# Window attention beside a GELU MLP: two one-bank PSUM tiles for the logits, one memset on another engine, and a new order of the pieces

## The chip, the cores and the metric

The kernel runs on one core of a Trainium2 chip. The metric is the device time of one execution in microseconds; several executions are timed and the median is given. One further execution is recorded by the hardware profiler; its trace is what the views below are taken from. Engines are called by their short names: PE (matmuls, and PEld for its weight loads), DVE, ACT, POOL and SP. SP and POOL, and now and then ACT, issue DMAs from their queues.

## The reference

For one sequence of 2048 rows of 640 columns, all in bf16:

```
xn  = layernorm(x)                                   # no gain or bias
q, k, v = split(xn @ wqkv)                           # 32 heads of 20 columns
logits[h, s, w] = q[h, s] . k[h, s - 2 w] / sqrt(20) # w = 0..7, masked where s - 2 w < 0
o[h, s] = sum_w softmax(logits)[h, s, w] * v[h, s - 2 w]
out = x + o @ wo + gelu(xn @ w1 + b1) @ w2 + b2      # w1: 640 x 1536, w2: 1536 x 640
```

## The kernel before

**Tiling.** The 2048 rows are four chunks n = 0..3 of 512 rows, each of four blocks of 128 rows. Normalised rows `xn` are turned so that the 640 columns lie on partitions (five tiles of 128). Everything on PE works on such turned chunks: 5 matmuls of 128x512 for each of 15 tiles of q, k, v (piece `pj`, line 333) and each of 12 tiles of the hidden layer (`f1`, line 614), and 12 + 5 matmuls for each of 5 output tiles (`t`, line 696). In chunk 0, q, k and v are made in halves and quarters of a chunk (`ga`, `gb`, `gd`, `ge`, `hj`; lines 346 and 377), so that work can begin before all of the chunk is loaded; in chunk 3 the outputs are not turned (`o`, line 652). ACT copies PE's results out of PSUM (`pc`, `hc`, `gc`), applies the GELU (`ge0_5` is tile 5 of chunk 0), makes `xn` for chunks 1 to 3 and takes the exponentials.

**Attention.** For each block j DVE multiplies q by eight shifted windows of k into `prod` (`qk`, line 430), folds the five column tiles by additions (`pa`, `pb`, lines 465 and 471), and PE sums each head's columns with a matrix of ones, `head_of`: piece `lg`, line 480, eight matmuls of 128x512 that make the logits tile `L`, 4 blocks x 32 heads on partitions, 8 windows x 128 rows in the free direction, 4 KB per partition. `L` is copied to SBUF as `e` (`cp`, lines 512 to 520); then come the mask (chunk 0 only), the maximum over windows and its subtraction (`m`, `mx`, DVE), the exponential (`ex`, ACT), the sum (`ss`, DVE), its reciprocal (`ri`, ACT), and the weights (`at`, DVE). DMAs on SP's queue spread the weights over the head's columns (`xe`, line 577). DVE multiplies them by windows of v (`av`, line 584) and adds up over windows (`ac`, partly by DMAs on POOL's queue, `ad`, `ot`).

**The softmax of chunk 0 goes in two parts** (`PARTS = (2, 1, 1, 1)`): each takes 64 of the 128 rows of every block. ACT copies the first part and DVE the second, and both parts of `L` reach over both halves of the windows, and so over both PSUM banks of the tile.

**PSUM.** Eight banks of 2 KB per partition: `psA` has four one-bank buffers (`pj`, `hj`, `f1`, most of `o`), `psO` two (`t`), and `psL` one buffer of two banks: the logits `L`, and at other times the idle matmuls that run before the data arrive, the bias transpose `tb`, and the first block of outputs in chunk 3.

**Loads at the start.** SP loads the rows of block 0, then wq, blocks 2 and 3, wk, chunk 1, wv and w1. ACT's queue loads block 1; DVE writes 16 columns of that block with zeros ahead of it (line 131), and the load has to wait for this write.

**What sets the order.** The program is written as some 600 small pieces, and `ORDER` lists them: each engine works through its own pieces in that order, and the queues of SP and POOL too. Nothing else reorders them. A piece waits by semaphores for what it reads, and for the buffer that it writes to be free. Pieces used in the text, all of chunk 0 unless said: `xn01a`, `xn01b` (DVE, the normalised block 1 in two parts), `tp01a` (PE, turns the first part), `lg0` (logits), `cp0a`, `cp0b`, `mask`; `pj1..` and `pj2..` (q, k, v of chunks 1 and 2) with the copies `pc1..`, `pc2..`; `hj210`, `hj211` with the copies `hc210`, `hc211`; `su`, `sq`, `rs`, `rc` (statistics of a later chunk's rows: two sums and the inverse root on ACT, `rc` the product -mean/std on DVE, line 252); `xn20`..`xn23` (normalised blocks of chunk 2, ACT, two buffers), `tc20`..`tc23` (DMA transposes of them, SP, line 291); `ut` and `ud` (the output tiles turned back and added to `out`).

Of the kernel before, what the change touches and what calls it, by code (L numbers as in the profile page):

```python
# [50 lines left out]
t002 xe00 ge0_9 pj123 pad21 su32 pb14 pj210 xe02 su31 pj203 xp1 pc210 su30 lg1 t042 pc203 av01 cp1b f10_10 ng3 f11_5  # L51
pj212 ge1_5 av00 ac01 pc123 f11_0 cp1a ge0_10 pj204 pad12 ge1_0 m1 pc212 ac00 pj211 sq32 av02 pj202 sq30 t003 pc211
pc204 pj221 pc202 mx1 pj223 av03 ex1 pj222 sq31 t043 pj214 ss1 pc222 pc221 f11_2 ac03 ri1 pj213 pc214 sq33 at1 pj220
ac02 pc213 xe11 rs3 xe13 pj201 pc220 xe10 rc3 ad01 pj224 pc201 xe12 pc223 ad00 pj200 f12_9 pc200 ot00 xn33 f12_3 ot01
xn31 tc33 av11 t004 tc31 t044 u00 pc224 t010 u04 ut00 av13 ac11 t011 xn32 t012 t013 ud00 f11_11 av12 t014 t030 u01
# [12 lines left out]
o330 ut24 ac32 o322 ud23 o313 ac33 o304 ad31 o331 ud24 o323 dl0 dh0 o314 ot31 dd0 o324 dl1 dh1 dd1 o332 dl2 o333 dh2
dd2 o334 ohi dl3 dlo dh3 dhi
# [4 lines left out]
def kernel(  # L74
# [44 lines left out]
    b_rt = consts.tile([P, P], BF16, name="b_rt")  # L119
    nc.gpsimd.memset(b_rt[:], 0.0)  # L120
# [10 lines left out]
    nc.vector.memset(x_sb[:, 1, 0:16], 0.0)  # L131
# [341 lines left out]
    def do_lg(n):  # L473
        L = psL.tile([P, W, P], F32, tag="L", name="L")
        tiles["L", n] = L
        ts = (range(KT), (0, 1, 4), (0, 4), (0,))[LEVEL[n]]
        for h in range(2):
            for t in ts:
                for j in range(BPC):
                    nc.tensor.matmul(  # L480
                        L[j * H : (j + 1) * H, W // 2 * h : W // 2 * (h + 1), :],
                        lhsT=head_of[:],
                        rhs=prod[:, j, W // 2 * h : W // 2 * (h + 1), t, :],
                        start=(t == 0),
                        stop=(t == ts[-1]),
                        skip_group_check=True,
                    )
# [24 lines left out]
    def do_cp(n, i):  # L512

        e = softmax_tile("e", n, [W, P], BF16)
        if PARTS[n] == 1:
            ws = slice(W // 2 * i, W // 2 * (i + 1))
            nc.scalar.copy(e[:, 0, ws, :], tiles["L", n][:, ws, :])
        else:
            cs, width = part(n, i)
            (nc.vector.tensor_copy if i else nc.scalar.copy)(e[:, i, :, :], tiles["L", n][:, :, cs])  # L520

# [335 lines left out]
```

## Time and profile before

| what | us |
|---|---|
| median of three runs | 206.66 (205.86 to 207.09) |
| the profiled execution | 205.97 |
| its span, from the first to the last instruction | 203.8 |
| DVE busy | 185.8 (91% of the span) |
| ACT busy | 128.9 (63%) |
| POOL busy | 29.3 (14%) |
| DMA moved | 27.31 MB, mean 134 GB/s |

The 2.2 us between the span and the execution's own time lie outside of the instructions. In a view's rows, times are microseconds from the start of the span: start, length, engine, line of the kernel, operation, tiles out<-in, shapes, how many instructions. A bracket at the end gives the idle time of the engine ahead of the row and what ended it. Matmuls overlap: a row's length reaches past the start of the next row, so that PE's pace is read from starts, not from lengths.

### The profile page before, as it was taken

What the parts mean: (1) busy time and instruction counts of PE and PEld (TensorE: products, weight loads), DVE (VectorE), ACT (ScalarE), POOL (GpSimd) and SP (SyncE); (2) the same over time, 40 slices, a digit from 0 to 9 for tenths busy, and PEclk for the clock granted to TensorE, in tenths of its full rate; (3) what the DMA queues carried; (4) which work ended last, traced back from release to release, by engine and by line L of the source; (5) the groups of instructions that cost most, each with busy time, mean ns of one, the idle gap of its engine ahead of it and who ended that gap; (6) DMA issues with size and microseconds to landing.
All of it is one profiled execution on the core that took longest, in us unless ns stands there. A gap on an engine that the chain in (4) does not pass through costs nothing.

```text
span 203.8 us, 2870 instructions
## 1 busy us (share of the span) xinstructions
PE 199.9 (98%) x1100; PEld 105.1 (52%) x1100; DVE 185.8 (91%) x160; ACT 128.9 (63%) x237; POOL 29.3 (14%) x34
## 2 busy tenths in 40 slices
PE   8999999999999999999999999999999999999994
PEld 3998456574544555444445544444434454444552
DVE  2889999699998999999999998999979999998871
ACT  5669899899896998657184445996379942230100
POOL 2000000000000400040420040000022713236210
PEclk9999999999999999999999999999999999999999
DMA  6997499900448781779399190003745899795851
GB/s 203 389 395 207 93 314 372 351 2 0 68 86 260 154 155 19 190 145 131 82 160 104 26 102 1 3 0 61 170 51 105 141 104 204 96 104 76 79 90 64
DMA packets 38430, 27.31 MB, mean 134 GB/s; under 512 B 25106, under 2 KB 34578, under 8 KB 38418
## 3 DMA queue, kind: packets, MB, share of 16 engines
q1 hardware_dynamic: 28016, 20.39, 35.3%
q0 software_dynamic: 10080, 6.56, 27.9%
q10 hardware_dynamic: 322, 0.20, 0.3%
q8 instruction: 8, 0.13, 0.3%
q14 instruction: 4, 0.03, 0.0%
HBM read 10.49 MB, written 4.59 MB: 74 GB/s over the span
## 4 chain that ended last, share of the span: by engine, by line
PE 84%; ACT 7%; DMA 4%; DVE 2%; SPq 1%; issue 1%
PE T L696 27%; PE hps L614 23%; PE pps L333 22%; PE lo L652 5%; DMA x_sb<-in_A_x_dram 4%; PE both L652 2%; DVE stats L213 2%; ACT xn L262 2%; PE gps L377 1%; PE hi L652 1%; ACT L170 1%; PE L L480 1%; ACT qT L392 1%; ACT e L543 1%; ACT kT L392 1%
## 5 line engine op out<-in xcount | busy, mean ns | idle before, releaser
L614 PE MATMUL hps<-xnT,w_sb 128*128 128x512 bf16 x240 | 56.2, 379 | 0.2 <-ACT hT L630 0.2
L430 DVE TENSOR_TENSOR prod<-qT,kT 128x5120 bf16<-128x5120 bf16 x16 | 44.6, 2821 | 1.3 <-ACT qT L397 1.0
L696 PE MATMUL T<-hT,w_sb 128*128 128x512 bf16 x180 | 44.6, 379 | 0.0
L614 PEld LDWEIGHTS <-w_sb 128*128 128x128 bf16 x240 | 23.4, 98 | 28.2 <-issue 0.5
L708 POOL DMA_DIRECT2D out_dram<-x_sb x15 | 20.8, 1485 | 65.7 <-DMA x_sb<-x_sb 65.6
L630 ACT ACTIVATE hT<-hps,bT 128x512 bf16<-128x512 f32 x36 | 23.7, 691 | 9.5 <-PE hps L614 9.3
L696 PEld LDWEIGHTS <-w_sb 128*128 128x128 bf16 x180 | 17.2, 98 | 20.9 <-issue 1.3
L584 DVE TENSOR_TENSOR prod<-vT,ax 128x5120 bf16<-128x5120 bf16 x8 | 22.4, 2821 | 1.9 <-PE L L480 1.1
L699 ACT ACTIVATE x_sb<-T,bT 128x512 bf16<-128x512 f32 x15 | 10.4, 693 | 21.6 <-PE T L696 19.2
L584 DVE TENSOR_TENSOR prod<-vT,x_sb 128x5120 bf16<-128x5120 bf16 x8 | 22.3, 2820 | 0.1
L595 POOL DMA_DIRECT2D prod<-prod x6 | 7.3, 1208 | 98.6 <-DVE prod L584 98.6
L170 ACT ACT_TABLE_LOAD x14 | 18.0, 1283 | 1.0 <-PEq L841 0.7
L471 DVE TENSOR_TENSOR prod<-prod 128x4096 bf16<-128x4096 bf16 x8 | 18.3, 2292 | 0.2
L333 PE MATMUL pps<-xnT,wq_sb 128*128 128x512 bf16 x75 | 18.5, 379 | 0.0
L696 PE MATMUL T<-oT,wo 128*128 128x512 bf16 x75 | 18.5, 379 | 0.0
L333 PE MATMUL pps<-xnT,wv_sb 128*128 128x512 bf16 x75 | 18.3, 379 | 0.0
L333 PE MATMUL pps<-xnT,wk_sb 128*128 128x512 bf16 x75 | 18.3, 379 | 0.0
L465 DVE TENSOR_TENSOR prod<-prod 128x4096 bf16<-128x4096 bf16 x8 | 18.1, 2288 | 0.1
L597 DVE TENSOR_TENSOR prod<-prod 128x2560 bf16<-128x2560 bf16 x10 | 14.6, 1485 | 0.0
L397 ACT CAST qT<-pps 128x512 bf16<-128x512 f32 x15 | 8.6, 582 | 7.2 <-PE pps L333 7.2
L333 PEld LDWEIGHTS <-wk_sb 128*128 128x128 bf16 x75 | 8.7, 118 | 7.7 <-issue 0.4
L333 PEld LDWEIGHTS <-wv_sb 128*128 128x128 bf16 x75 | 8.7, 117 | 7.6 <-issue 0.4
(96 smaller groups left out, 240.8 us busy)
## 6 DMA issues: line engine op xcount, KB each, us to landing
prod<-prod POOLq DMA_DIRECT2D x6, 640.0 KB, 6.5
ax<-attn SPq DMA_DIRECT2D x8, 256.0 KB, 4.3
x_sb<-attn SPq DMA_DIRECT2D x8, 256.0 KB, 4.2
w_sb<-in_B_w_dram SPq DMA_DIRECT2D x2, 960.0 KB, 11.3
out_dram<-x_sb SPq DMA_DIRECT2D x3, 640.0 KB, 5.0
w_sb<-in_B_w_dram SPq DMA_DIRECT2D x4, 480.0 KB, 7.2
out_dram<-x_sb POOLq DMA_DIRECT2D x15, 128.0 KB, 3.9
x_sb<-in_A_x_dram SPq DMA_DIRECT2D x2, 640.0 KB, 7.1
```

The costliest lines, as they stand in the source:

```text
L170: nc.scalar.preload_act_table_set(name)
L333: nc.tensor.matmul(ps[:], lhsT=wqkv_p[which][:, ti, to, :], rhs=xnT[:, ti, :], start=(ti == 0), stop=(ti == KT - 1),)
L430: nc.vector.tensor_tensor(out=prod[:, j], in0=q[:, :, at].unsqueeze(1).to_broadcast([P, W, KT, P]), in1=window(k, at), op=ALU.mult,)
L465: nc.vector.tensor_tensor(out=low, in0=low, in1=high, op=ALU.add)
L471: nc.vector.tensor_tensor(out=first, in0=first, in1=rows[:, :, t * P : (t + 1) * P], op=ALU.add)
L584: nc.vector.tensor_tensor(out=prod[:, j], in0=window(qkv_tile(n, 2), slice(j * P, (j + 1) * P)), in1=ax_view(n)[:, j, :, :].unsqueeze(2).t ...
L597: nc.vector.tensor_tensor(out=low, in0=low, in1=high, op=ALU.add)
L614: nc.tensor.matmul(ps[:], lhsT=w1_sb[:, ti, ft * P : (ft + 1) * P], rhs=tiles["xnT", n][:, ti, :], start=(ti == 0), stop=(ti == KT - 1),)
L630: nc.scalar.activation(hT, tiles["hps", n, ft][:], ACT.Gelu_apprx_tanh, bias=bT[:, ft : ft + 1], scale=1.0)
L652: nc.tensor.matmul(out_ps(bl, hi), lhsT=lhs, rhs=rhs[:, CH:D] if hi else rhs[:, 0:CH], start=pc == 0 and k == 0, stop=pc == 4 and k == len ...
L696: nc.tensor.matmul(ps[:], lhsT=lhs, rhs=rhs, start=pc == 0 and k == 0, stop=pc == 4 and k == len(srcs) - 1)
L708: nc.gpsimd.dma_start(dst, src, accum_op=ALU.add)
```

## The change

1. `psL` holds two tiles of one bank each, with the tags `L0` and `L1`. The logits of windows 0 to 3 are written into the one and those of windows 4 to 7 into the other. The idle matmuls use `L0`, the bias transpose `L1`, and the first outputs of chunk 3 one each.
2. A copy `cp` takes one of the two tiles, that is half of the windows, for all rows. In chunk 0 ACT takes `L0` and DVE `L1`; each writes both parts of `e`. In the other chunks ACT copies both, as before.
3. The zeros ahead of block 1's load are written by POOL, as its first memset of the kernel body, and no longer by DVE.
4. `ORDER` is another list of the same pieces.

The core of the diff:

```
+    nc.gpsimd.memset(x_sb[:, 1, 0:16], 0.0)
     nc.gpsimd.memset(b_rt[:], 0.0)
...
     load_x(0, 1)
-    nc.vector.memset(x_sb[:, 1, 0:16], 0.0)
     nc.scalar.dma_start(x_sb[:, 1, :], x_nb[:, 1, :])
...
-    idle = psL.tile([P, W, P], F32, tag="L", name="idle")
+    idle = psL.tile([P, CH], F32, tag="L0", name="idle")
...
-        tiles["tb"] = psL.tile([P, W, P], F32, tag="L", name="tb")
+        tiles["tb"] = psL.tile([P, CH], F32, tag="L1", name="tb")
...
     def do_lg(n):
-        L = psL.tile([P, W, P], F32, tag="L", name="L")
-        tiles["L", n] = L
         ts = (range(KT), (0, 1, 4), (0, 4), (0,))[LEVEL[n]]
         for h in range(2):
+            L = psL.tile([P, W // 2, P], F32, tag=f"L{h}", name="L")
+            tiles["L", n, h] = L
             for t in ts:
                 for j in range(BPC):
                     nc.tensor.matmul(
-                        L[j * H : (j + 1) * H, W // 2 * h : W // 2 * (h + 1), :],
+                        L[j * H : (j + 1) * H, :, :],
...
     def do_cp(n, i):
         e = softmax_tile("e", n, [W, P], BF16)
-        if PARTS[n] == 1:
-            ws = slice(W // 2 * i, W // 2 * (i + 1))
-            nc.scalar.copy(e[:, 0, ws, :], tiles["L", n][:, ws, :])
-        else:
-            cs, width = part(n, i)
-            (nc.vector.tensor_copy if i else nc.scalar.copy)(e[:, i, :, :], tiles["L", n][:, :, cs])
+        ws = slice(W // 2 * i, W // 2 * (i + 1))
+        copy = nc.vector.tensor_copy if i and PARTS[n] > 1 else nc.scalar.copy
+        copy(e[:, :, ws, :], tiles["L", n, i][:].rearrange("p w (a c) -> p a w c", a=PARTS[n]))
...
     def out_ps(bl, hi):
-        if bl == 0:
-            both = get("first", lambda: psL.tile([P, W, P], F32, tag="L", name="both"))[:].rearrange("p w c -> p (w c)")
-            return both[:, CH:D] if hi else both[:, 0:CH]
-        pool, tag = (psO, "o") if bl == BPC - 1 else (psA, "acc")
+        pool, tag = (psL, f"L{int(hi)}") if bl == 0 else (psO, "o") if bl == BPC - 1 else (psA, "acc")
```

Of the two lists, the stretches that the prediction speaks of: the start, the first GELUs, from the logits of chunk 0 to those of chunk 1, and the end.

```
-pad01 pad02 st00a st00 sum1 ho rs00 neg1 xn00a sq1 xn00b tp00a wa tp00b wb tc00a tc00b rs01 ga xn01a gb2 xn01b tp01a
-gb3 st02a tb tp01b tc01a gb4 st02 tc01b gd gc0
+pad01 pad02 st00a st00 sum1 ho rs00 neg1 xn00a sq1 xn00b tp00a tp00b tc00a wa rs01 wb tc00b ga xn01a xn01b tp01a gb2
+tc01a gb3 st03a tp01b gb4 st03 tc01b tb gd
...
-hc011 hj112 hc111 f10_2 hc112 xn13 f10_0 xn12 tc13 qk02 f10_1 tc12 ge0_0 f10_5 ldx qk03 f10_11 ge0_5 f10_3
+hj201 hc010 xn10 f10_5 b1 qk02 hc201 tc10 xn12 f10_3 tc12 f10_1 ldx qk03 ge0_5 f10_11 ge0_3 f10_0 f10_2 ge0_0
...
-sq22 lg0 pc114 ldo pj111 cp0b cp0a sq21 mask pj113 m0b pc103 m0a pj124 pc111 mx0a pc113 mx0b t000 pad11 qk11 pj120
-ex0b hj202 ex0a hj210 pc120 sq23 ss0a hj211 pc124 ss0b sq20 pj122 qk13 hc202 rs2 f10_7 hc211 pc122 t040 ri0b f10_8
-ri0a rc2 qk12 hc210 f10_4 f11_1 ge0_7 xn21 qk10 f11_3 ge0_4 tc21 xn20 pj121 ge1_3 tc20 t041 ge1_1 pa11 f11_9 ge0_8
-xn23 hj212 pc121 tc23 t001 xn22 pa10 f10_6 hc212 tc22 ge1_9 f11_10 ge0_6 at0a at0b f10_9 ge1_10 pb11 xe01 su33 xe03
-t002 xe00 ge0_9 pj123 pad21 su32 pb14 pj210 xe02 su31 pj203 xp1 pc210 su30 lg1
+sq22 pj114 xp2 pc102 lg0
+sq21 xp1 pj111 cp0b cp0a pc114 pj113 mask m0b pc112 m0a pad11 pc111 hj210 pc113 mx0b mx0a t040 qk13 t000 ex0b pj124
+sq23 pj122 ex0a ss0b pc124 pj123 sq20 ss0a hc210 f10_6 qk11 pc123 rs2 hj211 ri0b ri0a f11_10 pc122 hc211 at0b at0a
+f10_4 qk10 xe00 xe01 f10_8 ge1_10 ge0_4 pj121 ge0_6 rc2 qk12 xn23 hj202 f11_1 pc121 tc23 xn21 f10_7 hc202 tc21 ge1_1
+pa10 t001 ge0_8 f10_9 xe03 ge0_7 xn20 f11_9 pa11 xn22 tc20 t002 pj120 tc22 pb11 t041 pc120 ldo f11_3 pad21 ge0_9 su33
+f10_10 pb14 su32 xe02 t042 su31 pj203 ge0_10 ge1_9 lg1
...
-o330 ut24 ac32 o322 ud23 o313 ac33 o304 ad31 o331 ud24 o323 dl0 dh0 o314 ot31 dd0 o324 dl1 dh1 dd1 o332 dl2 o333 dh2
-dd2 o334 ohi dl3 dlo dh3 dhi
+t240 u22 ud13 ud20 ut21 ud14 av31 t241 t242 t243 t244 ac31 o303 u24 ud21 ut22 o312 ad30 o330 ud22 ut23 ut24 o313 ot30
+ud23 o320 ac32 o331 o321 ad31 o314 ot31 o304 dl1 ud24 o322 dl0 o323 dh0 dh1 dd0 o324 dd1 o332 dl2 o333 dh2 dd2 o334
+ohi dl3 dlo dh3 dhi
```

As built, the program has the same matmuls, DVE operations and DMAs as before, less the one memset on DVE and with one more on POOL, and 12 loads of ACT's function table in place of 14: the new order has two switches fewer between the GELU's table and that of the exponential and logarithm.

More of the change, by code (lines that the diff above doesn't have):

```diff
@@ L51 @@
[L51 to L55, printed above, removed]
@@ new lines @@
+tc01a gb3 st03a tp01b gb4 st03 tc01b tb gd st02a rs03 ge st02 gc0 xn03 hj101 rs02 gc1 xn02 gc4 tp03 st11a tp02 st10a
+hj100 st11 tc02 st10 tc03 hj102 st12a hc101 hj200 st12 hc102 hc100 st13a st13 hj112 hc200 hj111 rs1 rc1 qk00 xn13
+hj012 hj110 hc112 tc13 pk xn11 hj011 hc111 tc11 hc110 qk01 hj010 hc011 hc012 hj201 hc010 xn10 f10_5 b1 qk02 hc201 tc10
+xn12 f10_3 tc12 f10_1 ldx qk03 ge0_5 f10_11 ge0_3 f10_0 f10_2 ge0_0 xp0 pa00 ge0_11 pj101 ge0_1 ld2 ge0_2 pj100 pc101
+pa01 su20 pj110 pc100 pj104 pc110 pb01 su22 pj103 su21 pj102 pc104 su23 pb04 pj112 ng2 pc103 sq22 pj114 xp2 pc102 lg0
@@ new lines @@
+sq21 xp1 pj111 cp0b cp0a pc114 pj113 mask m0b pc112 m0a pad11 pc111 hj210 pc113 mx0b mx0a t040 qk13 t000 ex0b pj124
+sq23 pj122 ex0a ss0b pc124 pj123 sq20 ss0a hc210 f10_6 qk11 pc123 rs2 hj211 ri0b ri0a f11_10 pc122 hc211 at0b at0a
+f10_4 qk10 xe00 xe01 f10_8 ge1_10 ge0_4 pj121 ge0_6 rc2 qk12 xn23 hj202 f11_1 pc121 tc23 xn21 f10_7 hc202 tc21 ge1_1
+pa10 t001 ge0_8 f10_9 xe03 ge0_7 xn20 f11_9 pa11 xn22 tc20 t002 pj120 tc22 pb11 t041 pc120 ldo f11_3 pad21 ge0_9 su33
+f10_10 pb14 su32 xe02 t042 su31 pj203 ge0_10 ge1_9 lg1 f11_5 ge1_3 av01 pc203 pj201 pj214 pc201 cp1b av00 pj210 ac01
@@ new lines @@
+f12_4 xe23 t104 f12_8 pb31 u10 ge2_10 ut10 f13_10 t120 pb34 f13_6 ge2_8 ge3_10 f13_8 u11 ge2_4 ut11 ud10 lg3 ge3_8
+f12_1 av20 ge3_6 t121 ge2_1 t122 f12_11 av21 ac20 f12_7 ge2_11 pj320 f13_9 pc320 av23 ac21 cp3a f13_7 ge3_9 cp3b t230
+ge2_7 f12_5 m3 pj323 mx3 ge2_5 av22 t123 t124 ex3 t231 u12 t232 ss3 pc323 ut12 ud11 ud04 o300 ac23 o310 ri3 f13_11 at3
+o301 ac22 xe33 ge3_11 xe30 ge3_7 t200 pad32 ut13 ad20 t201 o311 ad21 t233 pj324 ot20 xe32 t202 pc324 ot21 ut14 t203
+av33 t204 t234 u20 ut20 t210 u23 ud12 av30 t211 xe31 t212 o302 t220 ac33 t221 t213 av32 t222 t214 t223 u21 t224 ac30
@@ L451, in do_tb @@
     def do_tb():
-        tiles["tb"] = psL.tile([P, W, P], F32, tag="L", name="tb")
-        nc.tensor.matmul(tiles["tb"][:, 0, 0 : FT + KT], lhsT=b_rt[:], rhs=ident[:, 0 : FT + KT], start=True, stop=True)
+        tiles["tb"] = psL.tile([P, CH], F32, tag="L1", name="tb")
+        nc.tensor.matmul(tiles["tb"][:, 0 : FT + KT], lhsT=b_rt[:], rhs=ident[:, 0 : FT + KT], start=True, stop=True)
     def do_b1():
-        nc.vector.tensor_copy(bT[:], tiles["tb"][:, 0, 0 : FT + KT])
+        nc.vector.tensor_copy(bT[:], tiles["tb"][:, 0 : FT + KT])
     def rows_of(a, b):
```

29 lines of the change are left out of this document (11 added, 18 removed).

## The prediction

> **What bounds the kernel now.** I read the busy shares first, then PE's timeline for places where it stands still, then what it stood for.
>
> ```profile
> PE 199.9 (98%) x1100; PEld 105.1 (52%) x1100; DVE 185.8 (91%) x160; ACT 128.9 (63%) x237; POOL 29.3 (14%) x34
> ...
> L170 ACT ACT_TABLE_LOAD x14 | 18.0, 1283 | 1.0 <-PEq L841 0.7
> ```
>
> PE is busy from the first transposes to the end, so a change can gain only what PE loses in gaps, and DVE at 91% stands close behind. PE's gaps show in the starts of its rows.
>
> ```profile
> 6.14 1.00 PE L346 MATMUL gps<-xnT,wq_sb 128*128 128x128 bf16 x15
> 6.98 0.28 PE L279 MATMUL tp<-ident,xn 128*128 128x128 bf16 x2
> ...
> 12.53 1.25 PE L377 MATMUL gps<-xnT,wq_sb 128*128 128x256 bf16 x10
> 13.62 1.25 PE L377 MATMUL gps<-xnT,wv_sb 128*128 128x256 bf16 x10
> ...
> 19.08 4.48 PE L614 MATMUL hps<-xnT,w_sb 128*128 128x512 bf16 x20
> 23.75 2.32 PE L614 MATMUL hps<-xnT,w_sb 128*128 128x512 bf16 x10 [0.19 <-ACT hT L630]
> ...
> 35.73 0.61 PE L480 MATMUL L<-prod,head_of 128*32 128x512 bf16 x8
> ...
> 41.27 1.80 PE L377 MATMUL gps<-xnT,wv_sb 128*128 128x256 bf16 x15
> 43.24 1.25 PE L377 MATMUL gps<-xnT,wv_sb 128*128 128x256 bf16 x10 [0.17 <-ACT vT L397]
> 44.53 1.24 PE L333 MATMUL pps<-xnT,wv_sb 128*128 128x512 bf16 x5
> 45.61 0.38 PE L614 MATMUL hps<-xnT,w_sb 128*128 128x512 bf16 x1
> ...
> 50.14 1.67 PE L614 MATMUL hps<-xnT,w_sb 128*128 128x512 bf16 x7
> 51.75 1.24 PE L333 MATMUL pps<-xnT,wv_sb 128*128 128x512 bf16 x5
> ...
> 62.22 0.81 PE L333 MATMUL pps<-xnT,wq_sb 128*128 128x512 bf16 x3
> 62.96 0.62 PE L480 MATMUL L<-prod,head_of 128*32 128x512 bf16 x8
> ...
> 149.74 0.62 PE L480 MATMUL L<-prod,head_of 128*32 128x512 bf16 x8
> ```
>
> The pace of unhindered matmuls: 128 columns (6.98 - 6.14) / 15 = 0.056, 256 columns (13.62 - 12.53) / 10 = 0.109, 512 columns (45.61 - 44.53) / 5 = 0.216. With it the gaps follow. 19.08 + 20 x 0.216 = 23.40, the next starts at 23.75: 0.35. 41.27 + 15 x 0.109 = 42.91 to 43.24: 0.33. 43.24 + 10 x 0.109 = 44.33 to 44.53: 0.20. 50.14 + 7 x 0.216 = 51.65 to 51.75: 0.10. Together **0.98 us**, 0.63 of it between the logits of chunk 0 (35.73) and those of chunk 1 (62.96). More than about 1 us is not to be had from PE. The rows of DVE and ACT tell why.
>
> ```profile
> 6.57 0.64 DVE L264 TENSOR_SCALAR xn<-x_sb,neg,rstd 128x256 bf16<-128x256 bf16 x2
> ...
> 33.24 2.29 DVE L471 TENSOR_TENSOR prod<-prod 128x4096 bf16<-128x4096 bf16 x1
> 36.39 0.69 DVE L520 CAST e<-L 128x512 bf16<-128x512 f32 x1 [0.86 <-PE L L480]
> 37.74 0.21 DVE L524 TENSOR_TENSOR e<-e,mask 32x128 bf16<-32x128 bf16 x1 [0.65 <-ACT e L520]
> ...
> 40.29 2.83 DVE L430 TENSOR_TENSOR prod<-qT,kT 128x5120 bf16<-128x5120 bf16 x1 [0.17 <-ACT kT L404]
> ...
> 47.61 0.15 DVE L252 TENSOR_TENSOR nmr<-neg,rstd 128x4 f32<-128x4 f32 x1
> ...
> 57.55 0.75 DVE L558 TENSOR_TENSOR attn<-e,rs 128x512 bf16<-128x512 bf16 x2
> 58.22 4.61 DVE L471 TENSOR_TENSOR prod<-prod 128x4096 bf16<-128x4096 bf16 x2
> ...
> 144.66 4.62 DVE L471 TENSOR_TENSOR prod<-prod 128x4096 bf16<-128x4096 bf16 x2
> ```
>
> ```profile
> 37.12 0.59 ACT L520 CAST e<-L 128x512 bf16<-128x512 f32 x1 [0.70 <-DVE e L520]
> ...
> 41.57 1.15 ACT L543 ACTIVATE e<-e 128x512 bf16<-128x512 bf16 x2
> 42.62 0.57 ACT L397 CAST vT<-pps 128x512 bf16<-128x512 f32 x1
> 43.09 0.83 ACT L232 ACTIVATE trash<-x_sb,neg 128x640 bf16<-128x640 bf16 x1
> 43.91 0.57 ACT L397 CAST vT<-pps 128x512 bf16<-128x512 f32 x1
> ...
> 50.21 0.91 ACT L262 ACTIVATE xn<-x_sb,nmr,rstd 128x640 bf16<-128x640 bf16 x1
> ```
>
> The gaps at 43.24 and 44.53 are PSUM buffers of `psA` that came free late: ACT copied q, k, v tiles (42.62 and 43.91) behind the exponentials, while PE waited. The two copies of chunk 0's logits ran one after the other: DVE 36.39 to 37.08, ACT 37.12 to 37.71, the mask at 37.74. And DVE has no room at the logits: it ends its fold for `lg0` at 33.24 + 2.29 = 35.53, for `lg1` at 58.22 + 4.61 = 62.83, 0.13 before PE starts them. **So a PE gap that goes ahead of `lg1` is worth only as much as DVE gets earlier too.**
>
> **The change part by part**, along PE's path.
>
> *Zeros on POOL.*
>
> ```profile
> 0.81 0.07 DVE L131 MEMSET x_sb<- 128x8 uint32 x1 [0.81 <-PEq L841]
> ...
> 0.74 0.20 POOL L120 MEMSET b_rt<- 128x128 bf16 x1 [0.29 <-POOLq L841]
> ```
>
> POOL begins at 0.74, DVE did at 0.81; 16 columns in place of the 128 of `b_rt` should take no longer than its 0.20. Block 1's load starts between 0.1 earlier and 0.1 later, and POOL's other constants up to 0.2 later, which the wait for the first rows covers (PE's first product starts at 6.14). I take 0.
>
> *Start.* `tp01a` now stands ahead of `gb2`. PE ends `ga` at 6.14 + 10 x 0.056 = 6.70, while `xn01a`, the first half of DVE's row at 6.57, is there at about 6.9. `gb2` filled this time before; now PE waits 0.25. Bounds: 0 and 0.3.
>
> *The gap at 23.75.* PE waited for the first GELU. In the new program one more `hj` group (`hj201`, 10 x 0.109 = 1.09) stands ahead of the GELU's matmuls, one `f1` fewer (5 x 0.216 = 1.08), and the buffer that `f10_11` takes is the one that ACT's copy `hc201` frees, ahead of the table load. The GELU is needed one group (1.08) later, and comes later by that copy alone (about 0.6): -0.35, bounds -0.35 and 0.
>
> *`lg0`.* PE arrives at 35.73 + 0.25 - 0.35 = 35.63. DVE's fold ends at 35.53 plus the bias copy `b1`, which now stands between two products (I take the 0.15 of the small row at 47.61), plus 0.13 as at `lg1`: 35.8. So `lg0` is DVE's: **+0.1**. The gap is given back here.
>
> *The copies.* They read different banks and wait for PE alone. From DVE's copy to the mask it was 1.35 (36.39 to 37.74); now the longer copy, 0.69, with some 0.05 behind it: DVE gains **0.6**. The price of the new form, a half of windows for all rows in place of all windows for half the rows, isn't in the trace; it has the same 512 elements in runs of 64 and I take 0, bounds 0 and another 0.69. In the Trainium skill, "PSUM — Partial Sum Buffer", section "PSUM bank collisions raise a hardware error", two engines must be kept off the same bank and quadrant, reads against reads included, while on different banks they run clean. By that rule the 0.70 ahead of ACT's copy goes altogether, and the trace agrees in that the two were kept apart when they shared banks.
>
> *The gaps between `lg0` and `lg1`.* `hj211` now waits for `hc210`. ACT's pieces from the end of `lg0` (36.4) to it are seven copies (0.5 each, starting to starting), a table load, two exponentials (1.15) and two squares (0.83): some 8 us with the load at 1.3, so 44.4. PE needs the buffer after 6 groups of five (6.5), `hj210` (1.1), two `t` pieces (1.3) and the logits (0.5), at 35.8 + 9.4 = 45.2. `pj122` waits for `pc111`, which stands ahead of the load, and `pj121` for a GELU one place earlier. I take all three gaps as gone, **-0.63**; by counting matmuls, 0.10 of work moves ahead of `lg1`. PE: 35.8 + 27.23 - 0.63 + 0.10 = 62.5. DVE: 62.83 + 0.1 - 0.6 + 0.13 = 62.46. `lg1` at **62.5 instead of 62.96**.
>
> *From there to the end.* The work is the same. At `lg3` DVE's fold ended at 149.28 with PE at 149.74; some 0.06 more may be lost there. In the last stretch the final additions `dl0`, `dh0` go behind `ot31`, which gives PE's last waits more room, and the last six pieces are the same. Two table loads fewer free ACT for some 2.6 us, but it waits for PE there: 0.
>
> Sum: 0.1 - 0.6 + 0.1 = **-0.4**: 205.97 becomes 205.57. The profiled execution lies 0.69 under the median, so the median is **206.3**.
>
> **The rivals.**
>
> *The copies gain nothing.* ACT comes to `cp0a` behind a square (`sq21`) and a copy; if it comes 0.6 late, the mask waits as before, DVE keeps 62.83 and `lg1` stays at 62.96. Then 206.66. For it: ACT's queue ahead of `lg0` is full of squares. Against: the square can begin half a microsecond ahead of the logits.
>
> *All gaps go.* No loss at the start, DVE earlier than I think: -0.98, hence 205.7, at the edge of 0.5%.
>
> *Slower: chunk 2's transposes meet the spreading of the weights.* Now `xn23` waits for DVE's `rc2`, which moved behind a product and the two `at`. From mask to that row it was 9.87; less 0.17, plus 2.83 and 0.75, it is 13.3, from a mask at 37.2: 50.5. Then `xn23`, a copy, `xn21` (0.91 + 0.57 + 0.91) until 52.9, `tc21`, `xn22` (it takes that buffer), `tc22`, then `pj203` on PE at 61.3 (35.8 plus 25.5 of work). And `xe00`, `xe01`, `xe03` are now issued just ahead of these transposes; before they came after.
>
> ```profile
> xnT<-xn SPq DMA_TRANSPOSE x12, 2.4
> ```
>
> ```profile
> L703 SPq DMA_TRANSPOSE x_sb<-x_sb x1: 2172/2172/2172, 143.7 to 143.7; - x1
> DMA to landing us min/median/max: 4.1/4.1/4.1
> ...
> L703 SPq DMA_TRANSPOSE x_sb<-x_sb x1: 2147/2147/2147, 160.1 to 160.1; - x1
> DMA to landing us min/median/max: 6.9/6.9/6.9
> ```
>
> Such a transpose took 2.4; one issued straight behind four weight spreads took 4.1, the slowest 6.9. With 2.4 twice the chain ends at 52.9 + 2.4 + 0.9 + 2.4 = 58.6 and PE waits for nothing. With 4.1 and 6.9 it ends at 64.8: 3.5 late, which less 0.4 is +3.1, a median of 209.8. It turns slower once both together exceed 52.9 + 0.9 to 61.7, 7.9 us. The Trainium skill, "DMA: Bandwidth & Descriptors", section "Issuing engines are not separate DMA queues", speaks for it: all DMAs end up on the same 16 engines and interleave. Against: only two spreads stand ahead, and a product of 2.8 us lies between them and `rc2`.
>
> **How the numbers follow.** Forecast 0.50 (206.3), nothing gained 0.13 (206.66), all gaps gone 0.20 (205.7), slower 0.17 (209.8). A measurement of this kernel tells about 0.5%, 1.03 us, from no change; the three runs shown lie 1.2 apart. Under 205.63 lie half of "all gaps" and an edge of the forecast: faster 0.20; slower 0.17; same 0.63. The range, 205.2 to 207.9, takes in the first three with 0.5 of scatter below and the unknown 0.69 of the copies and more above, and leaves out most of the slower case and the tails.
>
> **What would show it.** Right: `lg0` near 35.8, the two copies side by side with a mask about 0.8 after they begin, no gap on PE between `lg0` and `lg1`, `lg1` near 62.5, a span near 203.4. Wrong: a mask that waits for ACT; PE standing at `pj203` for a transpose; PE waiting on DVE's fold at `lg1` by more than 0.2.

## The result, and the profile after

| | before | changed |
|---|---|---|
| median of 11 executions each, on one chip | 206.09 (205.82 to 207.09) | **205.37** (205.27 to 205.99) |
| ratio, with its 95% interval | | **0.9958** [0.9942, 0.9974] |
| the profiled execution | 205.97 | 205.35 |
| its span | 203.8 | 203.2 |

All times are in microseconds. Timed twice more, each time on a chip beside the kernel before, the changed kernel gave 0.9974 [0.9965, 0.9982] and 0.998 [0.9954, 1.0006]. It is faster by some 0.2 to 0.4%, under the 0.5% that the prediction set as the least that it would tell from no change. Between the two traced executions lie 0.62 us, where 0.4 was forecast. Single executions that were plainly disturbed (1201.02 in the series of E1, 428.92 in that of E4, 210.18 in one of the kernel before) are left out of the comparisons.

On the page of the changed kernel, PE is as full as before and DVE does the same work; ACT loads two tables fewer.

```profile
PE 199.0 (98%) x1100; PEld 104.7 (52%) x1100; DVE 185.8 (91%) x159; ACT 127.8 (63%) x235; POOL 29.5 (14%) x35
...
L170 ACT ACT_TABLE_LOAD x12 | 15.4, 1283 | 0.9 <-PEq L835 0.7
```

PE's timeline of the changed kernel, at the places where the prediction read that of before (line numbers past 500 are a few lower than before: 611 is `f1`, 690 is `t`, 517 is `cp`):

```profile
6.00 0.75 PE L346 MATMUL gps<-xnT,wq_sb 128*128 128x128 bf16 x10
6.91 0.28 PE L279 MATMUL tp<-ident,xn 128*128 128x128 bf16 x2 [0.15 <-DVE xn L264]
...
9.47 1.25 PE L377 MATMUL gps<-xnT,wk_sb 128*128 128x256 bf16 x10
...
20.44 6.64 PE L611 MATMUL hps<-xnT,w_sb 128*128 128x512 bf16 x30
26.91 2.32 PE L333 MATMUL pps<-xnT,wq_sb 128*128 128x512 bf16 x10
...
33.39 2.32 PE L333 MATMUL pps<-xnT,wk_sb 128*128 128x512 bf16 x10
35.68 0.61 PE L480 MATMUL L<-prod,head_of 128*32 128x512 bf16 x8
...
61.22 1.24 PE L333 MATMUL pps<-xnT,wq_sb 128*128 128x512 bf16 x5
62.39 0.62 PE L480 MATMUL L<-prod,head_of 128*32 128x512 bf16 x8
...
149.06 0.62 PE L480 MATMUL L<-prod,head_of 128*32 128x512 bf16 x8
```

With the paces of the prediction (0.056, 0.109 and 0.216 a matmul): after `ga`, 6.00 + 10 x 0.056 = 6.56, PE stands 0.35 until `tp01a` at 6.91. The first GELUs no longer stop it: 20.44 + 30 x 0.216 = 26.92 is where the next row starts. From the end of `lg0` to `lg1` no gap is left; the row at 61.22 ends at 61.22 + 5 x 0.216 = 62.30, and what stays is 0.09 ahead of the logits. That 0.09 was there before the change too (61.79 + 1.08 = 62.87, and `lg1` at 62.96), as two more rows of PE in the profile of before show; the first of them is the mate of the row at 9.47.

```profile
9.24 1.25 PE L377 MATMUL gps<-xnT,wk_sb 128*128 128x256 bf16 x10
...
61.79 1.24 PE L333 MATMUL pps<-xnT,wq_sb 128*128 128x512 bf16 x5
```

DVE and ACT of the changed kernel, from the bias copy `b1` (line 456) over the logits of chunk 0 up to those of chunk 1:

```profile
20.93 0.17 DVE L456 COPY bT<-tb 128x17 f32<-128x17 f32 x1
21.01 5.55 DVE L430 TENSOR_TENSOR prod<-qT,kT 128x5120 bf16<-128x5120 bf16 x2
...
31.00 4.62 DVE L471 TENSOR_TENSOR prod<-prod 128x4096 bf16<-128x4096 bf16 x2
36.34 0.69 DVE L517 CAST e<-L 128x512 bf16<-128x512 f32 x1 [0.71 <-PE L L480]
37.13 0.21 DVE L521 TENSOR_TENSOR e<-e,mask 32x128 bf16<-32x128 bf16 x1
...
50.15 0.15 DVE L252 TENSOR_TENSOR nmr<-neg,rstd 128x4 f32<-128x4 f32 x1
...
57.48 4.62 DVE L471 TENSOR_TENSOR prod<-prod 128x4096 bf16<-128x4096 bf16 x2
```

```profile
36.44 0.58 ACT L517 CAST e<-L 128x512 bf16<-128x512 f32 x1
...
39.40 1.28 ACT L170 ACT_TABLE_LOAD   x1
...
55.89 0.92 ACT L262 ACTIVATE xn<-x_sb,nmr,rstd 128x640 bf16<-128x640 bf16 x1 [0.43 <-DMA xnT<-xn]
```

The two copies now run side by side, DVE from 36.34 and ACT from 36.44, and each takes as long as before (0.69 and 0.58). The mask follows 0.79 after DVE's copy begins, where it was 1.35. That is the rule which the prediction took from the Trainium skill ("PSUM — Partial Sum Buffer", "PSUM bank collisions raise a hardware error"): copies from different banks need no order, and the 0.70 ahead of ACT's copy is gone. DVE's fold for `lg0` ends at 35.62, 0.07 behind PE (33.39 + 10 x 0.216 = 35.55); that for `lg1` ends at 62.10, with PE at 62.30.

### The profile page after: what moved, and what is told of

It is laid out like the page before. It is cut to its first block, busy times and chain, and to the rows that moved or that the text cites. A ratio compares the mean times of both kernels' runs of the same rounds, so it can differ in the third digit from the quotient of the medians.

```text
span 203.2 us, 2868 instructions
## 1 busy us (share of the span) xinstructions
PE 199.0 (98%) x1100; PEld 104.7 (52%) x1100; DVE 185.8 (91%) x159; ACT 127.8 (63%) x235; POOL 29.5 (14%) x35
## 3 DMA queue, kind: packets, MB, share of 16 engines
q0 software_dynamic: 10080, 6.56, 27.2%
## 4 chain that ended last, share of the span: by engine, by line
PE 95%; ACT 1%; DMA 1%; DVE 0%; issue 0%
PE T L690 27%; PE hps L611 26%; PE pps L333 24%; PE lo L646 7%; PE gps L377 7%; PE hi L646 2%; DMA x_sb<-in_A_x_dram 1%; PE gps L346 1%; PE L L480 1%; PE tp L279 0%; ACT trash L232 0%; ACT trash L225 0%; ACT logv L244 0%; ACT rstd L247 0%; DVE xn L264 0%; DVE prod L658 0%
## 5 line engine op out<-in xcount | busy, mean ns | idle before, releaser
L690 PE MATMUL T<-hT,w_sb 128*128 128x512 bf16 x180 | 43.7, 379 | 0.0
L333 PE MATMUL pps<-xnT,wq_sb 128*128 128x512 bf16 x75 | 18.0, 379 | 0.0
L333 PE MATMUL pps<-xnT,wv_sb 128*128 128x512 bf16 x75 | 17.7, 379 | 0.0
L397 ACT CAST kT<-pps 128x512 bf16<-128x512 f32 x15 | 8.6, 588 | 10.6 <-PE pps L333 10.6
```

What stands on the lines that cost most here:

```text
L333: nc.tensor.matmul(ps[:], lhsT=wqkv_p[which][:, ti, to, :], rhs=xnT[:, ti, :], start=(ti == 0), stop=(ti == KT - 1),)
L690: nc.tensor.matmul(ps[:], lhsT=lhs, rhs=rhs, start=pc == 0 and k == 0, stop=pc == 4 and k == len(srcs) - 1)
```

## The experiments

The anchors of all traces, read from PE's timeline as above: the first product (`ga`), the time from there to `lg0`, from `lg0` to `lg1`, from `lg1` to `lg3`, and the span. From `lg3` to DVE's last operation every trace has the same 51.7.

| kernel | `ga` | to `lg0` | `lg0`-`lg1` | `lg1`-`lg3` | span | ratio to before |
|---|---|---|---|---|---|---|
| before | 6.14 | 29.59 | 27.23 | 86.78 | 203.8 | 1 |
| changed | 6.00 | 29.68 | **26.71** | 86.67 | 203.2 | 0.9958 [0.9942, 0.9974] |
| E1, order alone | 6.16 | 29.63 | **27.11** | 86.68 | 203.7 | 0.9998 [0.9987, 1.0009] |
| E2, banks alone | 6.23 | 29.32 | **26.61** | 86.78 | 203.3 | 0.9999 [0.9978, 1.002] |
| E2 again | 6.92 | 29.63 | **26.61** | 86.78 | 204.3 | 0.9983 [0.9957, 1.001] |
| changed, beside E2 again | 6.96 | 29.57 | 26.72 | 86.67 | 204.1 | 0.998 [0.9954, 1.0006] |
| E3, memset on DVE | 6.11 | 29.63 | 26.71 | 86.68 | 203.5 | 0.9973 [0.9962, 0.9983] |
| E4, `gb2` first | 6.38 | 29.61 | 26.71 | 86.67 | 203.5 | 0.9986 [0.9968, 1.0004] |
| E5, and `b1` earlier | 6.50 | 29.52 | 26.71 | 86.68 | 203.5 | 0.9978 [0.9944, 1.0013] |
| E7, spare work on DVE | 7.68 | 30.87 | **27.25** | 86.67 | 206.8 | 1.0022 [0.9997, 1.0047] |
| changed, beside F2, F5, F7 | 6.73 | 29.55 | 26.72 | 86.67 | 203.8 | 0.9974 [0.9965, 0.9982] |
| F2, wq in two loads | 6.33 | **31.21** | 26.71 | 86.68 | 205.5 | 1.0068 [1.0052, 1.0084] |
| F5, products first | 6.37 | **30.24** | 26.72 | 86.67 | 204.4 | 1.0018 [1.0006, 1.003] |
| F7, spare work again | 6.33 | 29.49 | **27.24** | 86.67 | 204.1 | 1.0012 [1.0003, 1.0021] |

The stretches behind `lg0` repeat to 0.01 or 0.02; `ga` does not, even with the same kernel (6.00, 6.73, 6.96), and the span follows it. So each cause is read from its own stretch, and the timed ratio tells whether it reaches the end. The changed kernel beside F2, F5 and F7 was expected at 205.4, with 26.71 from `lg0` to `lg1` whatever the start does; it gave 205.49 and 26.72.

### E1: the new order with the old tile

The theory: the order closes PE's gaps, but with the copies in a row DVE stays late, and `lg1` hardly moves. The rival: the order alone brings the gain. The edit puts the tile of two banks back into the changed kernel:

```
+        L = psL.tile([P, W, P], F32, tag="L", name="L")
+        tiles["L", n] = L
...
-        ws = slice(W // 2 * i, W // 2 * (i + 1))
-        copy = nc.vector.tensor_copy if i and PARTS[n] > 1 else nc.scalar.copy
-        copy(e[:, :, ws, :], tiles["L", n, i][:].rearrange("p w (a c) -> p a w c", a=PARTS[n]))
+        if PARTS[n] == 1:
+            ws = slice(W // 2 * i, W // 2 * (i + 1))
+            nc.scalar.copy(e[:, 0, ws, :], tiles["L", n][:, ws, :])
+        else:
+            cs, width = part(n, i)
+            (nc.vector.tensor_copy if i else nc.scalar.copy)(e[:, i, :, :], tiles["L", n][:, :, cs])
```

> The new order and the zeros on POOL, with the logits in one tile of two banks and the old copies. Theory (the copies and the order both take part; ACT's copy waits again for DVE's): ACT's copy starts at 37.1 instead of 36.44 and all that stands behind it on ACT is 0.6 later, the mask comes 0.55 later (37.7), DVE ends its fold for the logits of chunk 1 at 62.65 instead of 62.10, PE stands 0.3 for an eviction near 49.5, and those logits start near 62.8 instead of 62.39. Time: 0.4 us over the changed kernel, 0.3 under the one before. Rival A (the order alone makes the gain): as the changed kernel, logits of chunk 1 at 62.4. Rival B (the order gains nothing without the banks): as the kernel before.

Measured: 0.9998 [0.9987, 1.0009]. E1's ACT, DVE and PE:

```profile
37.18 0.58 ACT L520 CAST e<-L 128x512 bf16<-128x512 f32 x1 [0.49 <-DVE e L520]
```

```profile
37.80 0.21 DVE L524 TENSOR_TENSOR e<-e,mask 32x128 bf16<-32x128 bf16 x1 [0.65 <-ACT e L520]
...
58.22 4.62 DVE L471 TENSOR_TENSOR prod<-prod 128x4096 bf16<-128x4096 bf16 x2
```

```profile
46.32 3.47 PE L614 MATMUL hps<-xnT,w_sb 128*128 128x512 bf16 x15
49.96 1.24 PE L333 MATMUL pps<-xnT,wv_sb 128*128 128x512 bf16 x4 [0.17 <-ACT hT L630]
```

ACT waits for DVE's copy as before. PE's gaps at 43.24 and 44.53 are gone, but a new one stands behind a GELU that ACT reaches late: 46.32 + 15 x 0.216 = 49.56, and the next row starts at 49.96 (its x4 is a group of five with one record missing: the row behind it starts at 51.04, five paces on). That 0.40 is what `lg0`-`lg1` has over the 26.71 of the changed kernel. DVE's fold ends at 58.22 + 4.62 = 62.84, within a hundredth of where it ended before. Had PE no gap at all, `lg1` would still stand at 62.9. The theory had the places nearly right (37.1 for ACT's copy, 37.7 for the mask, a new gap near 49.5), but it put the fold's end at 62.65 and the time 0.3 under the kernel before. The fold came 0.19 later than that, and the time is that of rival B: no gain of the order alone can be told from zero.

### E2: the two tiles with the old order

The reverse: the program before, with the change's tiles and copies (the first two parts of the diff of the change) and nothing else.

```
-        L = psL.tile([P, W, P], F32, tag="L", name="L")
-        tiles["L", n] = L
...
+            L = psL.tile([P, W // 2, P], F32, tag=f"L{h}", name="L")
+            tiles["L", n, h] = L
...
+        copy = nc.vector.tensor_copy if i and PARTS[n] > 1 else nc.scalar.copy
+        copy(e[:, :, ws, :], tiles["L", n, i][:].rearrange("p w (a c) -> p a w c", a=PARTS[n]))
```

> The kernel before with two one-bank tiles for the logits and the new copies alone; old order, zeros on DVE. Theory (ACT comes 0.7 earlier to everything behind its copy, so the evictions that PE waited for at 43.24, 44.53 and 51.75 are in time): the gap of 0.35 at 23.75 stays, the three gaps behind the logits of chunk 0 go, the logits of chunk 1 start near 62.35 instead of 62.96, 0.6 us under the kernel before, about as fast as the changed one. Rival (the old order holds the evictions back whatever the copies do): the gaps at 43.24 and 44.53 stay, 0 to 0.2 us under the kernel before.

Measured: 0.9999 [0.9978, 1.002], an interval wider than the gain in question. The executions run from 205.43 to 208.14; their median is 205.73, beside 206.07 for the kernel before. The trace tells more. E2's ACT, DVE and PE:

```profile
36.14 0.59 ACT L517 CAST e<-L 128x512 bf16<-128x512 f32 x1
...
41.73 0.57 ACT L397 CAST vT<-pps 128x512 bf16<-128x512 f32 x1
```

```profile
36.22 0.69 DVE L517 CAST e<-L 128x512 bf16<-128x512 f32 x1 [0.86 <-PE L L480]
37.02 0.21 DVE L521 TENSOR_TENSOR e<-e,mask 32x128 bf16<-32x128 bf16 x1
...
57.33 4.61 DVE L471 TENSOR_TENSOR prod<-prod 128x4096 bf16<-128x4096 bf16 x2
```

```profile
41.10 2.89 PE L377 MATMUL gps<-xnT,wv_sb 128*128 128x256 bf16 x25
43.83 1.24 PE L333 MATMUL pps<-xnT,wv_sb 128*128 128x512 bf16 x5
```

The two gaps that the prediction had read as buffers freed late by ACT are gone in the *old* order: 25 matmuls run from 41.10 to 43.83 (25 x 0.109 = 2.73) without a stop. ACT no longer waits 0.70 for DVE's copy, so its copy of v, which stood at 42.62, now stands at 41.73 (0.18 of this is an earlier `lg0`). One repair serves both engines: DVE's fold ends at 61.94, PE comes at 62.07. Against the expectation, the gap of 0.35 at 23.75 was gone too; the run below shows that this was chance.

### E2 again, beside the changed kernel

Because of E2's wide interval, both kernels were timed on one chip.

> The two banks with the old order, timed once more because its first comparison, 0.9999 [0.9978, 1.002], told nothing while its trace lay 0.62 us shorter than the traced execution of before between the logits of chunk 0 and those of chunk 1 (26.61 against 27.23). If that stretch is the gain, these executions lie 0.5 to 0.6 us under the kernel before, a ratio of 0.997 to 0.998, as those of the changed kernel do. If the new order is needed for the gain, the ratio is 1.000 and the changed kernel beside it is 0.5 us faster.

> The changed kernel as it is, on the same chip as the kernel with the banks alone: 0.5 to 0.7 us under the kernel before (ratio 0.997). If the order adds nothing of its own, it lies within 0.2 us of the kernel with the banks alone; if the order carries the gain, 0.5 us under it.

Measured: 205.74 for the banks alone and 205.79 for the changed kernel, beside 206.1 for the one before: ratios of 0.9983 [0.9957, 1.001] and 0.998 [0.9954, 1.0006]. Both intervals touch 1 here, and no difference between the two kernels is seen. In the traces, the stretch from `lg0` to `lg3` says it more sharply: 27.23 + 86.78 = 114.01 before, 113.79 with the order alone, 113.39 with the banks alone (twice), 113.38 or 113.39 with both. Behind `lg0` the new order is worth 0.22 with the old tile and nothing with the new ones. Whether it is worth something ahead of `lg0` stays open: on the chip of E1 to E4, E3, which has the order and the tiles, had a median of 205.50 and E2 one of 205.73. In this second trace of E2, PE did stand 0.38 at the first GELU. The old order shows that gap in two traces of three, the new one in none but F5. Within the old order the gap costs 0.3 by `lg0` (29.63 from `ga` in the trace of E2 with it, 29.32 in the one without). The new order has no gap there and still takes 29.55 to 29.68: it loses the time again at other places (E4, E5 and the last section).

### E3: the memset back on DVE

```
-    nc.gpsimd.memset(x_sb[:, 1, 0:16], 0.0)
...
+    nc.vector.memset(x_sb[:, 1, 0:16], 0.0)
```

> The changed kernel with the zeros ahead of block 1's load written by DVE again. Theory: nothing, within 0.1 us; DVE's first statistics stay at 3.11. Rival (the earlier load of block 1 moves the start): the first statistics at 3.17, first transposes at 5.36, and 0.06 us more to the end.

Measured: 205.50 (205.47 to 205.59), 0.9973 [0.9962, 0.9983], and the same stretches behind `lg0`. DVE's first statistics stand at 3.25, neither the theory's 3.11 nor the rival's 3.17; in the three traces of the changed kernel they stand at 3.11, 3.27 and 3.40, so the scatter of the start hides what the memset does there. No effect on the time is seen, and one of 0.1 could not be seen: the three medians of the changed kernel are 205.37, 205.49 and 205.79.

### E4 and E5: filling the wait at `tp01a`, and `b1` out of the way

E4 puts `gb2` back between `ga` and `tp01a`. E5 does that as well and moves the bias copy `b1` from between two products into the place where DVE waits for an inverse root, because the prediction held DVE to be what `lg0` waits for.

```
-ga xn01a xn01b tp01a gb2
+ga xn01a gb2 xn01b tp01a
```

```
-hj112 hc200 hj111 rs1 rc1 qk00 xn13
+hj112 hc200 hj111 rs1 b1 rc1 qk00 xn13
...
-hc010 xn10 f10_5 b1 qk02 hc201 tc10
+hc010 xn10 f10_5 qk02 hc201 tc10
```

> The changed kernel with one piece moved in the order: the products gb2 stand ahead of the transposes tp01a again. Theory (DVE's fold decides when the logits of chunk 0 start): the wait of 0.32 on PE at 6.9 goes, PE comes 0.3 earlier to the logits of chunk 0, but they start at 35.6 to 35.7 as now, and the time is the same within 0.1 us. Rival (PE decides there): logits of chunk 0 at 35.4 and 0.3 us off the time.

> As the run before with gb2 ahead of tp01a, and the bias copy b1 on DVE moved from between two products into DVE's wait of 0.6 at 15.38. Theory: DVE's fold for the logits of chunk 0 ends 0.08 earlier, and these and everything behind start 0.08 earlier: 0.1 us under the changed kernel. Rival: PE's waits elsewhere take it back, 0.

Measured: 205.62 and 205.43, ratios 0.9986 [0.9968, 1.0004] and 0.9978 [0.9944, 1.0013]: no difference from the changed kernel that can be told. The starts of E4 and of E5:

```profile
6.38 1.18 PE L346 MATMUL gps<-xnT,wq_sb 128*128 128x128 bf16 x15
7.39 0.28 PE L279 MATMUL tp<-ident,xn 128*128 128x128 bf16 x2
```

```profile
6.50 1.03 PE L346 MATMUL gps<-xnT,wq_sb 128*128 128x128 bf16 x15 [0.29 <-DMA wq_sb<-in_A_wqkv_dram]
7.37 0.28 PE L279 MATMUL tp<-ident,xn 128*128 128x128 bf16 x2
```

The wait at `tp01a` is gone in E5 (6.50 + 15 x 0.056 = 7.34, and the row at 7.37) and down from 0.35 to 0.17 in E4 (7.22 and 7.39), but PE's first product stood later in these executions, in E5 behind the landing of wq, so that the forecast times of `lg0` can't be compared with the 35.99 and 36.02 measured. From `ga` to `lg0` it took 29.61 and 29.52, where the changed kernel has 29.68 in the trace with the wait: filling it is worth 0.07 to 0.16 by `lg0`, by one trace each. The two traces of the changed kernel in which wq landed late have no such wait and take 29.55 and 29.57. In E4 DVE is the next to be late: its fold ends at 35.94, with PE done at 35.85. In E5, with `b1` moved, both end at 35.93.

### E7 and F7: how much room has DVE?

An addition of 128x1280 is given to DVE between chunk 1's products and folds; nothing uses its result. If DVE sets `lg1`, nearly all of its length shows there; if PE does, only what exceeds DVE's room.

```
+        if (n, j) == (1, 2):
+            nc.vector.tensor_tensor(out=spare[:], in0=spare[:], in1=spare[:], op=ALU.add)
```

> The changed kernel with one addition of 128x1280 on DVE, of no use, behind the last product of chunk 1, ahead of the folds for its logits (about 0.8 us by the like of line 604); a zeroed tile for it is written by POOL at the start. Theory (DVE ends that fold only 0.2 before PE comes): the logits of chunk 1 start 0.5 to 0.6 later, 62.95, and the end moves by 0.4 to 0.6 us, since PE has no other idle time to give. Rival (DVE's share of 91% leaves room there): 0.

E7 was timed at 206.34, 1.0022 [0.9997, 1.0047], but its traced execution began with a wait of 1.37 for wq and ran at a granted clock of 0.99, so that its start can't be laid beside the others. F7 repeats it; the addition reads two blocks of rows of the input (128x1280) in place of the cleared tile.

> The changed kernel with one addition of 128x1280 on DVE, of no use, behind the last product of chunk 1, reading rows of x, without the zeroed tile. Theory (DVE ends the fold for chunk 1's logits only 0.2 before PE comes): from the logits of chunk 0 to those of chunk 1 27.25 instead of 26.71, and 0.5 us more to the end. Rival (room on DVE): 0.

F7: 206.27, 1.0012 [1.0003, 1.0021]. Its DVE and PE:

```profile
53.13 0.82 DVE L439 TENSOR_TENSOR spare<-x_sb 128x1280 bf16<-128x1280 bf16 x1
53.87 4.49 DVE L469 TENSOR_TENSOR prod<-prod 128x4096 bf16<-128x4096 bf16 x2
58.39 4.62 DVE L475 TENSOR_TENSOR prod<-prod 128x4096 bf16<-128x4096 bf16 x2
```

```profile
63.06 0.61 PE L484 MATMUL L<-prod,head_of 128*32 128x512 bf16 x8 [0.46 <-DVE prod L475]
```

The addition holds DVE for 53.87 - 53.13 = 0.74. DVE's fold ends at 63.01 and PE starts `lg1` at 63.06, with the wait written on DVE. `lg0`-`lg1` is 27.24 (27.25 in E7), 0.53 more than in the changed kernel, so DVE had 0.74 - 0.53 = 0.2 to spare, the 62.30 - 62.10 that its trace shows. And the 0.53 is not made up later: `lg1`-`lg3` stays at 86.67. The timed loss against the changed kernel on the same chip (206.27 to 205.49) is 0.78; 0.53 of it is located, the other 0.25 is not.

### F2: wq in two loads

The first product waits for wq in many traces. F2 loads it in two parts, so that PE may begin with the first.

```
-    load_w(0)
+    for ts in (slice(0, 2), slice(2, KT)):
+        nc.sync.dma_start(wqkv[0][:, ts, :], wqkv_v[:, ts, 0:D])
```

> The changed kernel with the load of wq in two DMAs, the two first of five row tiles and then three, so that PE's first ten products need the first DMA alone. Theory (in part of the executions the landing of wq holds these products): PE's first products at 6.0 in the profile, times spread less, median 0 to 0.2 us lower. Rival (the landing of wq decides nothing there; one more DMA to issue delays the rows behind it): 0 to 0.3 us slower.

Measured: 207.58, 1.0068 [1.0052, 1.0084], 2.1 slower than the changed kernel beside it, against the theory and beyond the rival's 0.3. The traced execution of F2 had a granted clock of 0.997; its PE:

```profile
7.96 0.75 PE L347 MATMUL gps<-xnT,wq_sb 128*128 128x128 bf16 x10 [0.64 <-DMA wq_sb<-in_A_wqkv_dram]
...
10.90 1.29 PE L378 MATMUL gps<-xnT,wk_sb 128*128 128x256 bf16 x10 [0.32 <-DMA wk_sb<-in_A_wqkv_dram]
```

```profile
wk_sb<-in_A_wqkv_dram SPq DMA_DIRECT2D x1, 800.0 KB, 8.2
wq_sb<-in_A_wqkv_dram SPq DMA_DIRECT2D x1, 480.0 KB, 6.2
wq_sb<-in_A_wqkv_dram SPq DMA_DIRECT2D x1, 320.0 KB, 3.8
```

The rows of the DMA view end with the time from issue to landing. The first part, 320 KB, lands after 3.8, but the second, issued half a microsecond later, takes 6.2, and wk, issued another microsecond later, takes 8.2. In the changed kernel beside it all of wq took 5.5 and wk 7.4, issued half a microsecond earlier than here. PE begins at 6.33 and then stands behind both: 1.66 of the 2.1 lie between `ga` and `lg0` (31.21 against 29.55). The executions of the two kernels do not overlap (207.03 to 207.96 against 205.35 to 206.0), so the loss is the split's; that it comes by these late landings is read from one trace.

### F5: DVE's first products earlier

F5 is E5 with chunk 0's first product ahead of `rc1`, the row statistics of chunk 1, so that DVE's products need not wait for them.

```
-rs1 b1 rc1 qk00 xn13 hj012 hj110 hc112 tc13 pk xn11 hj011 hc111 tc11 hc110 qk01 hj010 hc011
+rs1 b1 qk00 hj012 hj110 hc112 pk hj011 hc111 rc1 xn13 tc13 hc110 qk01 hj010 xn11 tc11 hc011
```

> The changed kernel with gb2 ahead of tp01a, b1 in DVE's wait, and the first product of q and k on DVE ahead of rc1, into the wait of 0.6 for chunk 1's statistics; xn13 and xn11 stand two copies later on ACT. Theory (DVE's fold decides when the logits of chunk 0 start, and PE has 0.3 to give with gb2 moved): fold ends 0.6 to 0.7 earlier, logits of chunk 0 and all behind 0.3 earlier, 0.3 us under the changed kernel where wq lands in time. Rival (chunk 1's rows then come too late for PE near 26.9, or ACT holds evictions back behind xn13): 0 or slower.

Measured: 206.49, 1.0018 [1.0006, 1.003], 1.0 slower than the changed kernel beside it. F5's ACT and PE:

```profile
17.89 0.92 ACT L262 ACTIVATE xn<-x_sb,nmr,rstd 128x640 bf16<-128x640 bf16 x1 [1.39 <-DVE nmr L254]
...
23.70 1.28 ACT L170 ACT_TABLE_LOAD   x1
```

```profile
25.73 2.32 PE L611 MATMUL hps<-xnT,w_sb 128*128 128x512 bf16 x10 [0.62 <-ACT hT L627]
```

`rc1`, a product of some 0.1, now stands behind a product of 2.8, and ACT, which needs it for the rows of chunk 1, waits 1.39. Its table load ahead of the first GELU comes 1.4 later (22.26 in the changed kernel), and the gap that the change had removed is back at twice its size: 20 matmuls from 20.63 would end at 24.95, and the next row starts at 25.73. So the rival held. An operation that is short on its own engine can be the one that another engine waits for.

## Why the prediction was right, point by point

Its mechanism holds: the copies side by side make DVE and ACT earlier, and PE's gaps ahead of `lg1` pay only as far as DVE gets earlier too. Along its steps:

- **Zeros on POOL, 0.** No effect is seen (E3).
- **Start, +0.25.** `wk`'s first row stands at 9.47 where it stood at 9.24: +0.23. The wait itself is 0.35, over the bound of 0.3, because `ga` happened to stand 0.14 earlier in this execution. By `lg0` it is worth some 0.1 (E4, E5).
- **The gap at 23.75, -0.35.** Held: gone in the changed kernel, and with the old order there in two traces of three. In the old order its absence is worth 0.3 by `lg0` (E2's two traces); the new order gives that back, as forecast.
- **`lg0`, +0.1, "the gap is given back here".** From the span's start -0.05 was measured (35.73 to 35.68). Counted from `ga` it is +0.09 (29.59 to 29.68), but `ga` stood 0.14 earlier by the scatter of the start and DVE's first product did not follow it (15.45 before, 15.46 after), so that this agreement is luck. DVE does come last, as forecast, but by 0.07 only: `b1` cost 0.08 (20.93 to 21.01) and not 0.15. The step that failed is the 0.13 behind DVE's fold, "as at `lg1`": the logits started 0.06 after the fold (35.62 to 35.68). At `lg1` of before, PE comes at 62.87 and the logits start 0.09 later, and this 0.09 is there too where DVE is done well ahead (by 0.2 at `lg1` of the changed kernel). So that pause is not DVE's; no run shows what it comes from.
- **The copies, -0.6 for DVE; the new form at no cost.** Held: the mask is 0.56 earlier against the start of DVE's copy (0.79 for 1.35), and the lengths are those of before. By the end of the fold for `lg1`, counted from `lg0`, DVE has gained 0.68 (27.10 to 26.42).
- **The three gaps, -0.63, and 0.10 of work moved ahead of `lg1`.** From `lg0` to `lg1` 26.71 was measured; the prediction had 62.5 - 35.8 = 26.7. The size was right, the cause half right: the step gave the gaps to the order ("`pj122` waits for `pc111`, which stands ahead of the load"). The order alone does close those at 43.24 and 44.53, but gets a new one (E1). E2 closes them in the old order, because ACT is some 0.7 earlier without its wait for DVE's copy.
- **From there to the end, 0, with 0.06 that may be lost.** Measured -0.11 from `lg1` to `lg3`. The work that moved ahead of `lg1` is missing behind it; the sum kept the +0.10 and forgot its return.

The account of the traces: -0.05 at `lg0`, -0.52 to `lg1`, -0.11 to `lg3`, 0 from there: -0.68 in place of -0.4, of which the tail beyond DVE's last operation leaves -0.62. What repeats in every trace of the changed kernel and of E2 is the -0.62 or -0.63 behind `lg0`; the rest moves with the start. Of the 0.9 between the forecast of 206.3 and the 205.37, 0.57 is the level of before: it was taken as the 206.66 of three executions, 0.69 over the trace, while the eleven beside the changed kernel gave 206.09. The other 0.3 is the gain, 0.72 between the medians in place of 0.4. That the range still held the time, by 0.17 at its lower end, is owed to the 0.5 of scatter that it allowed there, and is luck.

Of the rivals, "the copies gain nothing" fell with ACT's start at 36.44: its square ended just in time. "All gaps go" was nearest in time (205.7), though the start did lose. The slower one had a mechanism that shows in the trace. These are chunk 2's transposes in the changed kernel, those issued between 50 and 58:

```profile
L291 SPq DMA_TRANSPOSE xnT<-xn x4: 1222/1590/1990, 51.3 to 57.5; - x4
...
DMA to landing us min/median/max: 2.7/3.4/4.1
```

The last two (`tc20`, `tc22`), whose landing the view shows, took 4.1 and 2.7, where all four took 2.4 before; a spread of the weights was issued at 54.65, just ahead of them. That DMAs from all queues interleave on the same engines is what the prediction had cited from the Trainium skill ("DMA: Bandwidth & Descriptors", "Issuing engines are not separate DMA queues"). The longer times agree with it, but no run takes the spread away. The chain of the prediction is `tc21` and `tc22`. `tc21` was issued at 53.4 and ACT, waiting for it, went on at 55.89 (the wait of 0.43 above; before the change it was 0.98): some 2.5. `tc22` was issued at 57.5 and landed by some 60.2, 1.0 before `pj203` starts at 61.22. Together they took some 5.2, under the 7.9 at which it would have turned.

## What to carry to other kernels

When two engines copy halves of one result out of PSUM, cut the result by banks, not by the parts that follow: the wait that goes frees both engines, and here that gives all of the gain that repeats, with either order. Before a gap on the busiest engine is counted as a gain, look at the second engine's own arrival at the same place; closing the gap pays only up to there (in E1 `lg1` could not come before DVE's 62.9; in F7 0.53 of 0.74 showed). Count work that an order moves over a mark on both sides of that mark.

## What the runs showed beyond this

The start of this kernel scatters more than the change is worth. The load of wq, 800 KB issued at 1.2, in the changed kernel and in E7:

```profile
wq_sb<-in_A_wqkv_dram SPq DMA_DIRECT2D x1, 800.0 KB, 4.8
```

```profile
wq_sb<-in_A_wqkv_dram SPq DMA_DIRECT2D x1, 800.0 KB, 6.4
```

It landed after 4.6 to 6.4 in the thirteen traces that load it as one, and where it took 5.3 or more, PE's first product is shown to wait for it. It is not the only such load. In the changed kernel beside E2 again, `lg0` stood at 36.53 in place of 35.68 and the span was 204.1 in place of 203.2, more than the whole difference to the kernel before; and there PE stood for wv too, which took 10.2 (9.1 in the first trace):

```profile
wv_sb<-in_A_wqkv_dram SPq DMA_DIRECT2D x1, 800.0 KB, 10.2
```

```profile
11.75 1.80 PE L377 MATMUL gps<-xnT,wk_sb 128*128 128x256 bf16 x15
13.61 1.29 PE L377 MATMUL gps<-xnT,wv_sb 128*128 128x256 bf16 x10
```

11.75 + 15 x 0.109 = 13.39, so PE stood 0.22; the load was issued at 3.36 and landed at 13.56. In the profile, the chain of waits that ends in `lg0` passes through this landing, and not through that of wq, in both later traces of the changed kernel. The new order asks for wv at 12.76 (first trace), the old one at 13.62, so late loads cost the new order here what they don't cost the old one: E2 again, with wv after 10.1, runs through. What decides the landing wasn't found.
